# Talking-heads attention with two mixers: the odd key block of the second mix kept whole on one column half, and the first mix put ahead of the score product

## The chip, the cores and the metric

The kernel runs on one core of a Trainium2 chip. The metric is device time in microseconds (us), the time of the slowest core, here the only one. The engines are TensorE (PE, with its weight loads PEld), VectorE (DVE), ScalarE (ACT), GpSimd (POOL) and SyncE (SP), which issues the DMAs.

## The reference

Three stages follow each other, all in float32. The change touches the first alone.

```python
# attention: 2 batches, 12 heads, 448 rows, head size 64; w_pre and w_post are 12 x 12
scores = scale * np.matmul(q, k.transpose(0, 1, 3, 2))
scores = np.einsum('bhij,hg->bgij', scores, w_pre)          # first mix, over heads
scores = scores - np.max(scores, axis=-1, keepdims=True)
attn = np.exp(scores)
attn = attn / (np.sum(attn, axis=-1, keepdims=True) + 1e-09)
attn = np.einsum('bhij,hg->bgij', attn, w_post)             # second mix, over heads
x = np.matmul(attn, v)                                      # then heads side by side: 448 x 768
# mixer 1: u = x + token mixing (448 -> 256 -> 448); x = u + relu(u @ w_ch1) @ w_ch2   (768 -> 1536 -> 768)
# mixer 2: gelu(x @ w_in) in two halves, the second normalised and mixed over tokens,
#          product of the halves @ w_out, plus x
```

## The kernel before, in words

**Attention** takes about the first 190 us. A batch's 448 query rows are cut in four chunks of 120, 120, 120 and 88 rows. A chunk is worked through in steps of 20 rows: 46 steps in all, of which the last of each batch has 10 rows (`ne` is 1 there, else 2). A step's 20 rows are four groups of 5 rows; a group times 12 heads fills 60 partitions. So TensorE is used as four quarters of 64x64: row half (which half of the partitions the operands lie in) times column half (which half of the partitions of PSUM is written). Four matmuls, one for each quarter, run side by side.

For a step i, in the order in which the code writes it (the engines keep this order; a wait holds up all that stands behind it on its engine):

- `qk` (L319): the score product of two heads of the next chunk, 4 matmuls of 448 columns into a PSUM pair of the pool `psM`, which ACT copies to `S`. Six of these are spread over a chunk's steps.
- `b_pre(i + 2)` (L362): the first mix. Its operand `P` comes by DMA out of `S`, turned so that heads lie on partitions (`b_dma`, issued 5 steps ahead). 4 matmuls of 448 columns into the pool `psB`.
- `b_max(i + 2)` (DVE, tile `nm`), `b_norm(i + 1)` (POOL: `rc`, `rr` and two `wt`, w_post scaled by one over the sums).
- `b_post(i)` (L400): the second mix, which also turns the data: the exponentials `E` are the stationary operand, cut in blocks of 64 keys, `wt` (60 columns) the moving one. 448 keys are seven blocks. Blocks 0 to 5 go in twos, one to each column half. For the seventh both column halves do half the heads each: two matmuls of 30 columns where the others have 60. This makes 32 matmuls in a full step.
- `b_exp(i + 2)` (ACT, two activations into `E`), `b_turn(i)` (DVE, in three steps ACT: PSUM to `AT`).
- in some steps `av` (L431), the product of a chunk's `AT` with `v`, for three pairs of heads: 18 matmuls that contract over all 128 partitions, and then 6 that contract over 64 for the seventh key block, whose `AT` and `v` lie on the low half of the partitions for heads 0 to 5 and on the high half for heads 6 to 11. Two bank halves `x` of the PSUM pair take the two groups of heads. ACT and DVE copy the result to `xT`, with an interleaving of rows. There are 16 of these.
- the DMAs, and `pump(1)` (L179): one step of the conversion of later weights, which puts single instructions on ACT, DVE or POOL.

`psM` has two buffers, used in turn by `qk`, `post`, `av` and `xps` (transposes in the last five steps). So a `qk` in a step behind a plain step needs the buffer of the `qk` before it, which is free when ACT has copied that one to `S`.

**The rest** (about 194 us to the end) is the two mixers, dense matmuls in 3-term float32r products; nothing of it changes.

A float32 matmul stands in the trace as two MATMUL records, each with a weight load: 32 matmuls are 64 records.

Of the kernel before, what the change touches and what calls it, by code (L numbers as in the profile page):

```python
# [8 lines left out]
F32 = mybir.dt.float32  # L9
# [5 lines left out]
AF = mybir.ActivationFunctionType  # L15
ALU = mybir.AluOpType
AX = mybir.AxisListType
PSUM = bass.MemoryType.PSUM

LD, LP = 5, 2  # L20
# [10 lines left out]
def tile_kernel(ctx, tc, q, k, v, w_pre, w_post, w_tok1, w_tok2, w_ch1, w_ch2,  # L31
                w_u, w_v, g_ln, w_sg, b_sg, w_out, out):
    nc = tc.nc
    B, D, H, S = 2, 64, 12, 448
    P = 128
    NP = H // 2
# [7 lines left out]
    IB = 10  # L44
    TILES = P // IB
    CH = [(0, 120), (120, 120), (240, 120), (360, 88)]
# [8 lines left out]
    xT = xpool.tile([P, NCC, T], F32, name="xT")  # L55
# [188 lines left out]
    for o in GATE_ORDER.split():  # L244
        j = int(o[1])
# [40 lines left out]
    atp = actx.enter_context(tc.tile_pool(name="atp", bufs=1))  # L286
    ap_ = actx.enter_context(tc.tile_pool(name="attn", bufs=1))
# [12 lines left out]
    NQ = NP // QG  # L300

    def load_v(b, g):
        t = vn[b, g] = ap_.tile([P, 14 * D], F32, tag=f"vn{g}", name=f"vn{b}_{g}")
        nc.sync.dma_start(out=t, in_=v[b, :, g])

    def load_q(b, c, g, eng=nc.sync):
# [55 lines left out]
    def b_pre(i):  # L362
        ne = steps[i][3]
        ps = st[i]["pre"] = pair(f"pre{i}", psB)
        for r, cols in enumerate(HALVES):
            for e in range(ne):
                rs = slice(64 * e, 64 * e + 64 - PAD * e)
                nc.tensor.matmul(ps[cols, e, :S], lhsT=wp[rs], rhs=ring[(2 * i + r) % NP_BUFS][rs], start=True, stop=True)  # L368
# [26 lines left out]
            st[i]["w"].append(wt)  # L395

    AT = {}
    NG = (NK // 2) * H + H // 2

    def b_post(i):  # L400

        b, c, p, ne = steps[i]
        if p == 0:
            AT[b, c] = atp.tile([P, NG, CH[0][1]], F32, tag="AT", name=f"AT{b}_{c}", bufs=2)
        ps = st[i]["ps"] = pair(f"post{i}")
        for e in range(ne):
            E, wt = st[i]["e"][e], st[i]["w"][e]
            for s in range((NK + 1) // 2):
                for x, cols in enumerate(HALVES):
                    t = min(2 * s + x, NK - 1)  # L410
                    w = slice(0, HW) if 2 * s + 1 < NK else slice(x * HW // 2, (x + 1) * HW // 2)
                    o = e * 256 + s * HW
                    for r in range(2):
                        rs = slice(64 * r, 64 * r + HW)
                        nc.tensor.matmul(ps[cols, r, o:o + w.stop - w.start], lhsT=E[rs, t * 64:(t + 1) * 64],  # L415
                                         rhs=wt[rs, w], start=True, stop=True)

    def b_turn(i, copy):

        b, c, p, ne = steps[i]  # L420
        src = st[i]["ps"].rearrange("p r (e x) -> p (r e) x", e=2)[:, ::3 - ne, :NG * HB]
        dst = AT[b, c][:, :, 2 * IB * p:2 * IB * p + 2 * ne * HB]
        dst, src = dst.rearrange("p g (a i) -> p a g i", i=HB), src.rearrange("p a (g i) -> p a g i", i=HB)
        if i < NB - 1:
            copy(dst, src)  # L425
        else:
            nc.scalar.copy(dst[:, :1], src[:, :1])
            nc.vector.tensor_copy(dst[:, 1:], src[:, 1:])
        st[i] = None

    def av(b, c, hps):  # L431

        s0, n = CH[c]
        nb = n // IB
        rest = n - nb * IB
        cols = IB * (nb + (rest > 0))
        NH = NK // 2
        ps = pair(f"av{b}_{c}_{hps[0]}")
        at = AT[b, c]
        sides = [[hp for hp in hps if hp // (NP // 2) == x] for x in range(2)]  # L440

        def into(hp, x, j):
            o = sides[x].index(hp) * cols
            return ps[HALVES[j], x, o:o + cols]

        for x in range(2):
            for hp in sides[x]:
                for s in range(NH):
                    for j in range(2):
                        nc.tensor.matmul(into(hp, x, j), lhsT=vn[b, hp // 2][:, ((hp % 2 * 2 + j) * NH + s) * D:][:, :D],  # L450
                                         rhs=at[:, s * H + 2 * hp + j, :cols], start=(s == 0 and hp == sides[x][0]),
                                         stop=False, skip_group_check=True)
        for m in range(max(map(len, sides))):
            for x in range(2):
                if m < len(sides[x]):
                    hp = sides[x][m]
                    g = hp % (NP // 2)
                    for j in range(2):
                        nc.tensor.matmul(into(hp, x, j), lhsT=vn[b, g][HALVES[x], (4 * NH + j) * D:][:, :D],
                                         rhs=at[HALVES[x], NH * H + 2 * g + j, :cols], start=False, stop=True,  # L460
                                         skip_group_check=True)

        t0 = s0 + b * S
        for hs, x, copy in zip(sides, range(2), (nc.scalar.copy, nc.vector.tensor_copy)):
            dst = xT[:, hs[0]:hs[-1] + 1]
            src = ps[:, x, :len(hs) * cols].rearrange("p (c k) -> p c k", k=cols)
            copy(dst[:, :, t0:t0 + nb * IB].rearrange("p c (i j) -> p c j i", j=nb),
                 src[:, :, :nb * IB].rearrange("p c (j i) -> p c j i", i=IB))
            if rest:
                h = rest // 2  # L470
                copy(dst[:, :, t0 + nb * IB:t0 + n].rearrange("p c (i r) -> p c r i", r=2),
                     src[:, :, nb * IB:].rearrange("p c (r i) -> p c r i", i=HB)[:, :, :, :h])

    CW = C // 2

# [79 lines left out]
    AT_ACT = (-5, -3, 3)  # L555
    TURNS_AT = {(-1, 0), (4, 0), (-3, 1), (-2, 1), (0, 1), (1, 1), (4, 1)}

    AVS = ((0, 1, 3), (2, 4, 5))
    END = NB - LD
    LAST_AV = (0, 1)  # L560
    todo = []
# [299 lines left out]
    banks = {}  # L861
# [53 lines left out]
def layouts(q, k, v, w_pre, w_post, moe_w_tok1, moe_w_tok2, moe_w_ch1, moe_w_ch2,  # L915
# [28 lines left out]
    def spread(a):  # L944

        n = a.shape[-1]
        full, rest = n // 10, n % 10 // 2
        t = np.zeros((*a.shape[:-1], 128), a.dtype)
        rows = t[..., :120].reshape(*a.shape[:-1], 10, 12)
        rows[..., :full] = a[..., :10 * full].reshape(*a.shape[:-1], 10, full)  # L950
        if rest:
            rows[..., :rest, full:full + 2] = a[..., 10 * full:].reshape(*a.shape[:-1], rest, 2)
        t[..., :120] = rows.reshape(*a.shape[:-1], 120)
        return t

    def tokens(w):
# [10 lines left out]
    vr = v.reshape(B, 2, H // 4, 2, S, D)[..., whole:, :].transpose(0, 1, 4, 2, 3, 5).reshape(B, 128, H // 4, 2 * D)  # L967
    vt = np.concatenate([vt.reshape(B, 128, H // 4, -1), vr], -1)
# [57 lines left out]
```

## Time and profile before

| | before |
|---|---|
| runs | 509.75, 505.27, 509.64 us; median 509.64 |
| the profiled execution | 511.61 us, of which the span of the trace is 509.8 |
| PE busy, of the span | 485.2 us, 95% |
| DVE, ACT, POOL busy | 342.6, 236.5, 208.7 us |
| instructions | 14006, of which MATMUL 6010 and LDWEIGHTS 6010 |
| DMA | 63.84 MB, mean 125 GB/s |

The share of busy time is a mean over stages with different limits; the attention has to be read by itself. "Issue" in a list of waits is time in which an engine waited for nothing that the profile shows.

### The profile page before, as it was taken

Reading aid. Unit: us, or ns where it says so; the run is one execution under the profiler, and the core shown is the slowest. Engines: PE = TensorE matmul, PEld = TensorE weight load, DVE = VectorE, ACT = ScalarE, POOL = GpSimd, SP = SyncE. Lnnn points to the kernel's source line nnn. Section 1 sums busy time; section 2 is a strip of 40 time slices with the busy share of each in tenths; the row PEclk is TensorE's granted clock in tenths of the full one; section 3 lists DMA queues with packets and bytes.
Section 4 is the critical chain, followed back from the end, with each engine's and each line's share of the span. In section 5 each row is a group of like instructions: output and inputs, shape, how many; then the busy total and the mean of one; then the engine's idle time right before and its main releaser. Section 6 shows DMA issues by size and latency. Waiting matters only on the chain.

```text
span 509.8 us, 14006 instructions
## 1 busy us (share of the span) xinstructions
PE 485.2 (95%) x6010; PEld 411.8 (81%) x6010; DVE 342.6 (67%) x452; ACT 236.5 (46%) x457; POOL 208.7 (41%) x292
## 2 busy tenths in 40 slices
PE   9987999989799889999999999999999999999997
PEld 5455677756577569999999999999999998888896
DVE  4574566657365645963657687789887964897882
ACT  3675576576466434462434443333332345454320
POOL 2355256365355420284123322444554434258400
PEclk9999999999899999999999999999999999999999
DMA  6788364455523500310234343353432323103122
GB/s 225 231 227 232 139 219 154 153 200 179 171 112 139 205 4 2 125 63 27 98 103 145 125 143 105 123 165 101 149 123 88 119 73 124 32 0 123 68 85 109
DMA packets 26306, 63.84 MB, mean 125 GB/s; under 512 B 2900, under 2 KB 19844, under 8 KB 26244
## 3 DMA queue, kind: packets, MB, share of 16 engines
q1 hardware_dynamic: 26100, 62.75, 37.0%
q8 instruction: 47, 0.77, 0.6%
q10 hardware_dynamic: 144, 0.20, 0.1%
q14 instruction: 15, 0.12, 0.1%
HBM read 40.83 MB, written 2.75 MB: 85 GB/s over the span
## 4 chain that ended last, share of the span: by engine, by line
PE 89%; issue 4%; ACT 2%; DVE 2%; DMA 1%; POOL 1%; SPq 0%; POOLq 0%; ACTq 0%
PE qk L328 8%; PE post L415 8%; PE av L450 6%; PE c1ps L632 6%; PE c2ps L632 6%; PE pre L368 6%; PE c2ps L634 6%; PE c1ps L634 6%; PE c2ps L633 6%; PE c1ps L633 6%; PE ups L633 2%; PE ups L632 2%; PE ups L634 2%; PE vps L634 2%; PE vps L633 2%
## 5 line engine op out<-in xcount | busy, mean ns | idle before, releaser
L156 POOL TENSOR_TENSOR wl<-cv,wh 128x768 fp32r<-128x768 f32 x28 | 52.6, 1878 | 132.0 <-ACT wh L153 100.6
L415 PEld LDWEIGHTS post<-wt,E 60*64 60x64 f32 x2880 | 54.3, 138 | 31.8 <-issue 23.6
L381 ACT ACTIVATE E<-pre,nm 128x448 f32<-128x448 f32 x90 | 56.3, 632 | 37.3 <-DVE nm L373 33.4
L415 PE MATMUL post<-wt,E 60*64 60x60 f32 (+1 forms) x2880 | 56.3, 221 | 10.5 <-issue 8.3
L373 DVE TENSOR_REDUCE nm<-pre 128x2 f32<-128x896 f32 (+1 forms) x46 | 49.1, 1068 | 24.0 <-PE pre L368 22.2
L135 DVE SCALAR_TENSOR_TENSOR cv<-raw,cv 128x768 uint32<-128x768 uint32 (+2 forms) x44 | 53.1, 1207 | 1.2
L328 PE MATMUL qk<-kn,qn 64*64 64x448 f32 x384 | 50.0, 565 | 3.2 <-issue 1.9
L632 PE MATMUL c1ps<-uh,wh 128*128 128x448 f32 x144 | 52.3, 363 | 0.0
L632 PE MATMUL c2ps<-r1h,wh 128*128 128x448 f32 x144 | 52.3, 363 | 0.0
L368 PE MATMUL pre<-P,wp 64*64 64x448 f32 (+1 forms) x360 | 50.7, 547 | 1.7 <-ACT E L381 1.1
L634 PE MATMUL c2ps<-r1h,wl 128*128 128x448 f32 x144 | 52.2, 362 | 0.0
L634 PE MATMUL c1ps<-uh,wl 128*128 128x448 f32 x144 | 52.2, 362 | 0.0
L633 PE MATMUL c1ps<-ul,wh 128*128 128x448 f32 x144 | 51.8, 360 | 0.0
L633 PE MATMUL c2ps<-r1l,wh 128*128 128x448 f32 x144 | 51.8, 360 | 0.0
L425 DVE COPY AT<-post 128x840 f32<-128x840 f32 (+1 forms) x42 | 44.0, 1047 | 9.7 <-PE post L415 9.6
L113 ACT ACTIVATE cv<-raw 128x768 f32<-128x768 f32 (+2 forms) x44 | 36.1, 821 | 26.9 <-POOL wl L156 19.9
L388 POOL TENSOR_SCALAR rc<-sm 128x2 f32<-128x2 f32 (+1 forms) x46 | 10.5, 229 | 90.2 <-ACT E L381 89.7
L333 ACT COPY S<-qk 128x896 f32<-128x896 f32 x42 | 38.0, 905 | 17.4 <-PE qk L328 15.4
L137 DVE SCALAR_TENSOR_TENSOR cv<-raw,cv 128x768 uint32<-128x768 uint32 (+2 forms) x44 | 40.3, 915 | 1.0
L153 ACT CAST wh<-cv 128x768 fp32r<-128x768 f32 x28 | 23.4, 835 | 34.8 <-DVE cv L137 33.9
L655 DVE SCALAR_TENSOR_TENSOR r1l<-c1ps,r1h 128x448 fp32r<-128x448 f32 x24 | 15.0, 624 | 30.6 <-ACT r1h L653 30.6
L450 PE MATMUL av<-AT,vn 128*64 128x120 f32 (+1 forms) x576 | 32.5, 266 | 2.0 <-issue 1.9
(148 smaller groups left out, 1035.3 us busy)
## 6 DMA issues: line engine op xcount, KB each, us to landing
P<-S SPq DMA_DIRECT2D x88, 210.0 KB
raw<-in_w_ch_dram SPq DMA_DIRECT2D x24, 768.0 KB
raw<-in_w_v_dram SPq DMA_DIRECT2D x6, 512.0 KB
raw<-in_w_u_dram SPq DMA_DIRECT2D x4, 768.0 KB
raw<-in_w_out_dram SPq DMA_DIRECT2D x6, 512.0 KB
qn<-in_q_dram SPq DMA_DIRECT2D x15, 192.0 KB
kn<-in_k_dram SPq DMA_DIRECT2D x12, 224.0 KB
vn<-in_v_dram SPq DMA_DIRECT2D x6, 448.0 KB
```

What stands on the lines that cost most here:

```text
L135: nc.vector.scalar_tensor_tensor(fi, lo, 29, fi, op0=ALU.logical_shift_right, op1=ALU.bitwise_or)
L156: nc.gpsimd.tensor_tensor(dst[1], f, f32(dst[0]), op=ALU.subtract)
L328: nc.tensor.matmul(ps[cols, j, :S], lhsT=qn[b, c, i // QG][rows, i % QG, cols], rhs=KX[b, i][rows], start=True, stop=True)
L368: nc.tensor.matmul(ps[cols, e, :S], lhsT=wp[rs], rhs=ring[(2 * i + r) % NP_BUFS][rs], start=True, stop=True)
L373: nc.vector.tensor_reduce(out=st[i]["nm"][:, :ne], in_=st[i]["pre"][:, :ne, :S], axis=AX.X, op=ALU.max, negate=True)
L381: nc.scalar.activation(t, st[i]["pre"][:, e, :S], AF.Exp, bias=st[i]["nm"][:, e:e + 1], scale=1.0, accum_out=sm[:, e:e + 1])
L415: nc.tensor.matmul(ps[cols, r, o:o + w.stop - w.start], lhsT=E[rs, t * 64:(t + 1) * 64], rhs=wt[rs, w], start=True, stop=True)
L425: copy(dst, src)
L450: nc.tensor.matmul(into(hp, x, j), lhsT=vn[b, hp // 2][:, ((hp % 2 * 2 + j) * NH + s) * D:][:, :D], rhs=at[:, s * H + 2 * hp + j, :cols], ...
L632: nc.tensor.matmul(ps, lhsT=lh, rhs=rh, start=(start and i == 0), stop=False)
L633: nc.tensor.matmul(ps, lhsT=lh, rhs=rl, start=False, stop=False)
L634: nc.tensor.matmul(ps, lhsT=ll, rhs=rh, start=False, stop=(stop and i == n - 1))
```

## The change

The second mix: the seventh key block is no longer cut by heads. With `e` for the two halves of a step's rows, block seven of half `e` goes whole (60 columns) to column half `e`; in a step with `ne` of 1, to column half `r`. The matmuls of a full step become 28. `AT` gets a layout of 84 groups of 60 columns (before 42 of 120) of the same size; `b_turn` copies as many elements as before, and in the two short steps splits them between ACT and DVE in four copies.

The product with v: block seven of a pair of heads now lies on the low partitions for half the chunk's rows and on the high ones for the other half. So its 6 matmuls of up to 120 columns become 12 of up to 60. Half of them stand ahead of the 18 full ones (each row half writing one bank half) and half behind (with bank halves exchanged). Between the two a tiny POOL memset (`turned_at`, 128x8) waits for the first ones, and the first of the second ones waits for it. The 18 full matmuls read their moving operand in two runs of 60 columns instead of one of 120. The tile of `v` grows from 14x64 to 16x64 columns, as block seven is stored for both halves. The pairs of heads of the two calls become (0, 1, 2) and (3, 4, 5), ACT always copies two pairs and DVE one, in plain rows; q's columns are ordered differently in memory to fit.

In a step `b_pre(i + 2)` stands ahead of the first `qk`.

```diff
-        t = vn[b, g] = ap_.tile([P, 14 * D], F32, tag=f"vn{g}", name=f"vn{b}_{g}")
+        t = vn[b, g] = ap_.tile([P, 16 * D], F32, tag=f"vn{g}", name=f"vn{b}_{g}")
...
+    turned_at = ap_.tile([P, 8], F32, name="turned_at")
+    NH = NK // 2
+    GM = NH * H
+    NG = 2 * GM + H
...
+        def mix(e, r, x, t, o):
+            rs = slice(64 * r, 64 * r + HW)
+            nc.tensor.matmul(ps[HALVES[x], r, o:o + HW], lhsT=st[i]["e"][e][rs, t * 64:(t + 1) * 64],
+                             rhs=st[i]["w"][e][rs, :HW], start=True, stop=True)
+
         for e in range(ne):
-            E, wt = st[i]["e"][e], st[i]["w"][e]
-            for s in range((NK + 1) // 2):
-                for x, cols in enumerate(HALVES):
-                    t = min(2 * s + x, NK - 1)
-                    w = slice(0, HW) if 2 * s + 1 < NK else slice(x * HW // 2, (x + 1) * HW // 2)
...
+            for s in range(NH):
+                for x in range(2):
                     for r in range(2):
...
+                        mix(e, r, x, 2 * s + x, (e * NH + s) * HW)
+        for r in range(2):
+            for e in range(ne):
+                mix(e, r, e if ne == 2 else r, NK - 1, 2 * NH * HW)
...
+        def rests(turned, fence=None):
+
+            mms = []
+            for m in range(len(sides[0])):
+                for e in range(2):
+                    x = e ^ turned
+                    if m < len(sides[x]):
+                        hp = sides[x][m]
+                        o = m * cols + e * half
+                        for j in range(2):
+                            mms.append(nc.tensor.matmul(
+                                ps[HALVES[j], x, o:o + half],
+                                lhsT=vn[b, hp // 2][HALVES[e], (4 * NH + hp % 2 * 2 + j) * D:][:, :D],
+                                rhs=at[HALVES[e], 2 * GM + 2 * hp + j, :half],
+                                start=(not turned and m == 0), stop=turned, skip_group_check=True))
+            if fence:
+                tc.add_manual_dep(mms[0].ins, fence.ins.name, SYNC, reason="banks change rows")
+            return mms
+
+        mms = rests(False)
+        fence = nc.gpsimd.memset(turned_at, 0.0)
+        for mm in mms[-4:]:
+            tc.add_manual_dep(fence.ins, mm.ins.name, SYNC, reason="banks change rows")
         for x in range(2):
-            for hp in sides[x]:
+            for m, hp in enumerate(sides[x]):
                 for s in range(NH):
                     for j in range(2):
...
+                                         rhs=main[:, :, s * H + 2 * hp + j, :half], start=False, stop=False,
...
+        rests(True, fence)
...
-    AVS = ((0, 1, 3), (2, 4, 5))
+    AVS = ((0, 1, 2), (3, 4, 5))
...
+        if ahead:
+            b_pre(i + LP)
         if due:
             qk(*due.pop(0))
-        if ahead:
-            b_pre(i + LP)
```

The first place is TensorE in step 6 (score product `qk`, first mix `pre` of step 8, second mix `post`). Before:

```order
L328 MATMUL qk_2_5_639<-kn_5_115,qn_2_1_227 64x448 x4
L368 MATMUL pre_645<-P_93,wp 64x448 x2
L368 MATMUL pre_645<-P_94,wp 64x448 x2
L415 MATMUL post_661<-wt_0_594,E_0_568 64x60 x12
L415 MATMUL post_661<-wt_0_594,E_0_568 64x30 x4
L415 MATMUL post_661<-wt_1_596,E_1_570 64x60 x12
L415 MATMUL post_661<-wt_1_596,E_1_570 64x30 x4
```

In the change:

```order
L369 MATMUL pre_616<-P_93,wp 64x448 x2
L369 MATMUL pre_616<-P_94,wp 64x448 x2
L329 MATMUL qk_2_5_621<-kn_5_116,qn_2_1_228 64x448 x4
L413 MATMUL post_638<-wt_0_575,E_0_549 64x60 x12
L413 MATMUL post_638<-wt_1_577,E_1_551 64x60 x12
L413 MATMUL post_638<-wt_0_575,E_0_549 64x60
L413 MATMUL post_638<-wt_1_577,E_1_551 64x60
L413 MATMUL post_638<-wt_0_575,E_0_549 64x60
L413 MATMUL post_638<-wt_1_577,E_1_551 64x60
```

The eight matmuls of 30 columns are gone, four of 60 stand at the end; the score product stands directly ahead of the second mix.

The second place is TensorE behind that second mix, where the product with v follows. Before:

```order
L450 MATMUL av_0_0_700<-AT_0_280,vn_0_123 64x120 x12
L450 MATMUL av_0_0_700<-AT_0_280,vn_1_385 64x120 x6
L459 MATMUL av_0_0_700<-AT_0_280,vn_0_123 64x120 x4
L459 MATMUL av_0_0_700<-AT_0_280,vn_1_385 64x120 x2
L328 MATMUL qk_3_0_736<-kn_0_101,qn_3_0_575 64x448 x4
```

In the change:

```order
L460 MATMUL av_0_0_673<-AT_0_281,vn_0_124 64x60 x2
L460 MATMUL av_0_0_673<-AT_0_281,vn_1_378 64x60 x2
L460 MATMUL av_0_0_673<-AT_0_281,vn_0_124 64x60 x2
L477 MATMUL av_0_0_673<-AT_0_281,vn_0_124 64x120 x12
L477 MATMUL av_0_0_673<-AT_0_281,vn_1_378 64x120 x6
L460 MATMUL av_0_0_673<-AT_0_281,vn_1_378 64x60 x2
L460 MATMUL av_0_0_673<-AT_0_281,vn_0_124 64x60 x4
L369 MATMUL pre_715<-P_95,wp 64x448 x2
```

Six short matmuls stand on each side of the 18, where six long ones stood behind them.

The third place is POOL in the same step, the chain that scales w_post (`rc`, `rr`, `wt`) for the next step and for the one behind it. In the change:

```order
L389 TENSOR_SCALAR rc_629<-sm_608 128x2
L391 TENSOR_TENSOR rr_631<-rc_629,mone 128x2
L395 TENSOR_SCALAR wt_0_633<-wd_post,rr_631 128x60
L395 TENSOR_SCALAR wt_1_635<-wd_post,rr_631 128x60
L470 MEMSET turned_at 128x8
L389 TENSOR_SCALAR rc_729<-sm_667 128x2
```

The memset is new; before, the second `rc` follows the `wt` directly.

## Rows read from the trace of the kernel before

**Rows 1.** Attention: busy us (instructions) of PE, PEld, DVE, ACT, POOL; clock, DMA, GB/s.

```profile
19.30:194.00 174.70, 156.18 (x4274) 116.64 (x4276) 103.54 (x123) 105.17 (x249) 81.37 (x190) 0.97 0.50 164
```

**Rows 2.** Chain that ended last, 145 to 155 us: start, us, what.

```profile
145.49 0.75 PE qk L328 x6
...
147.90 0.78 PE qk L328 x6
148.69 0.75 PE pre L368 x8
...
150.47 0.98 PE qk L328 x8
...
152.20 0.90 PE post L415 x64
153.10 2.00 PE av L450 x36
155.10 0.46 PE av L459 x10
```

**Rows 3.** ACT's timeline, 149 to 153 us: start, us, what, idle before.

```profile
149.51 0.90 ACT L333 COPY S<-qk 128x896 f32<-128x896 f32 x1
150.71 0.63 ACT L381 ACTIVATE E<-pre,nm 128x448 f32<-128x448 f32 x1 [0.30 <-issue]
...
151.95 0.90 ACT L333 COPY S<-qk 128x896 f32<-128x896 f32 x1
```

**Rows 4.** Waits of PE: for what, us in total, times, longest.

```profile
PE post L415 <- issue: 8.3, 8, 3.1
PE av L459 <- issue: 2.1, 3, 1.3
PE av L450 <- issue: 1.9, 2, 1.1
PE qk L328 <- issue: 1.9, 1, 1.9
...
PE qk L328 <- ACT S L333: 1.0, 1, 1.0
```

**Rows 5.** The page's DMA queue of instructions: packets, MB, share of 16 engines.

```profile
q8 instruction: 47, 0.77, 0.6%
```

**Rows 6.** PE between two issue waits: us, busy (matmul records), clock, DMA.

```profile
124.05:128.70 4.65, 3.76 (x127) 1.00 0.86 254
```

**Rows 7.** Second mix (L415), two stretches: us, PE busy (records begun), PEld, clock.

```profile
72.60:72.97 0.37, 0.34 (x24) 0.34 (x24) 1.00 0.87 237
72.60:73.06 0.46, 0.43 (x32) 0.43 (x32) 1.00 0.89 265
```

**Rows 8.** PE's timeline in one product with v.

```profile
87.05 2.07 PE L450 MATMUL av<-AT,vn 128*64 128x120 f32 x36
89.04 0.53 PE L459 MATMUL av<-AT,vn 64*64 64x120 f32 x10
...
89.50 0.92 PE L328 MATMUL qk<-kn,qn 64*64 64x448 f32 x6
```

**Rows 9.** DVE's timeline, 149 to 152 us.

```profile
149.53 1.09 DVE L373 TENSOR_REDUCE nm<-pre 128x2 f32<-128x896 f32 x1 [0.37 <-PE pre L368]
150.54 1.05 DVE L425 COPY AT<-post 128x840 f32<-128x840 f32 x1
```

**Rows 10.** Chain that ended last, 45 to 52 us.

```profile
45.74 3.12 issue
...
50.13 1.56 PE qk L328 x7
```

**Rows 11.** The stretch behind that wait; its granted clock is 0.55.

```profile
48.50:52.30 3.80, 3.44 (x53) 2.51 (x57) 1.06 (x1) 0.57 (x1) 3.03 (x4) 0.55 0.84 242
```

**Rows 12.** POOL's timeline around the product with v of the rows above.

```profile
84.94 1.93 POOL L131 TENSOR_SCALAR cv<-cv 128x512 f32<-128x512 f32 x1
...
88.09 0.60 POOL L394 TENSOR_SCALAR wt<-wd_post,rr 128x60 f32<-128x60 f32 x2
```

More of the change, by code (lines that the diff above doesn't have):

```diff
@@ L17 @@
 AX = mybir.AxisListType
+SYNC = mybir.DependencyInfo(mybir.DependencyClass.Sync, mybir.DependencyReason.DATA)
 PSUM = bass.MemoryType.PSUM
@@ L397, in tile_kernel @@
     AT = {}
-    NG = (NK // 2) * H + H // 2
+    turned_at = ap_.tile([P, 8], F32, name="turned_at")
+    NH = NK // 2
+    GM = NH * H
+    NG = 2 * GM + H
     def b_post(i):
@@ L403, in b_post @@
         if p == 0:
-            AT[b, c] = atp.tile([P, NG, CH[0][1]], F32, tag="AT", name=f"AT{b}_{c}", bufs=2)
+            AT[b, c] = atp.tile([P, NG, CH[0][1] // 2], F32, tag="AT", name=f"AT{b}_{c}", bufs=2)
         ps = st[i]["ps"] = pair(f"post{i}")
+        def mix(e, r, x, t, o):
+            rs = slice(64 * r, 64 * r + HW)
+            nc.tensor.matmul(ps[HALVES[x], r, o:o + HW], lhsT=st[i]["e"][e][rs, t * 64:(t + 1) * 64],
+                             rhs=st[i]["w"][e][rs, :HW], start=True, stop=True)
@@ L406, in b_post @@
         for e in range(ne):
-            E, wt = st[i]["e"][e], st[i]["w"][e]
-            for s in range((NK + 1) // 2):
-                for x, cols in enumerate(HALVES):
-                    t = min(2 * s + x, NK - 1)
-                    w = slice(0, HW) if 2 * s + 1 < NK else slice(x * HW // 2, (x + 1) * HW // 2)
-                    o = e * 256 + s * HW
+            for s in range(NH):
+                for x in range(2):
                     for r in range(2):
-                        rs = slice(64 * r, 64 * r + HW)
-                        nc.tensor.matmul(ps[cols, r, o:o + w.stop - w.start], lhsT=E[rs, t * 64:(t + 1) * 64],
-                                         rhs=wt[rs, w], start=True, stop=True)
+                        mix(e, r, x, 2 * s + x, (e * NH + s) * HW)
@@ L418, in b_turn @@
+        for r in range(2):
+            for e in range(ne):
+                mix(e, r, e if ne == 2 else r, NK - 1, 2 * NH * HW)
     def b_turn(i, copy):
         b, c, p, ne = steps[i]
[L421 to L424, printed above, removed]
+        src = st[i]["ps"][:, :, :NG * HB].rearrange("p r (g i) -> p r g i", i=HB)
@@ L425, in b_turn @@
+        dst = AT[b, c][:, :, 2 * HB * p:2 * HB * p + ne * HB].rearrange("p g (r i) -> p r g i", i=HB)
+        if ne == 2:
             copy(dst, src)
         else:
-            nc.scalar.copy(dst[:, :1], src[:, :1])
-            nc.vector.tensor_copy(dst[:, 1:], src[:, 1:])
+            main = dst[:, 0, :2 * GM].rearrange("p (e g) i -> p e g i", e=2)
+            for r, rows in enumerate(HALVES):
+                copy = (nc.scalar.copy, nc.vector.tensor_copy)[r]
+                copy(main[:, r], src[:, r, :GM])
+                copy(dst[rows, 0, 2 * GM:], src[rows, r, 2 * GM:])
@@ L433, in av @@
         s0, n = CH[c]
[L434 to L437, printed above, removed]
+        half = -(-n // IB) * HB
+        cols = 2 * half
         ps = pair(f"av{b}_{c}_{hps[0]}")
         at = AT[b, c]
[L440 to L444, printed above, removed]
+        main = at[:, :2 * GM].rearrange("p (e g) c -> p e g c", e=2)
@@ new lines, in av @@
+        sides = hps[:-1], hps[-1:]
+        def rests(turned, fence=None):
[15 more added lines that the diff above has]
+            return mms
@@ L446, in av @@
+        mms = rests(False)
+        fence = nc.gpsimd.memset(turned_at, 0.0)
+        for mm in mms[-4:]:
+            tc.add_manual_dep(fence.ins, mm.ins.name, SYNC, reason="banks change rows")
         for x in range(2):
-            for hp in sides[x]:
+            for m, hp in enumerate(sides[x]):
                 for s in range(NH):
                     for j in range(2):
-                        nc.tensor.matmul(into(hp, x, j), lhsT=vn[b, hp // 2][:, ((hp % 2 * 2 + j) * NH + s) * D:][:, :D],
-                                         rhs=at[:, s * H + 2 * hp + j, :cols], start=(s == 0 and hp == sides[x][0]),
-                                         stop=False, skip_group_check=True)
@@ L453, in av @@
[L453 to L460, printed above, removed]
+                        nc.tensor.matmul(ps[HALVES[j], x, m * cols:(m + 1) * cols].rearrange("p (e c) -> p e c", e=2),
+                                         lhsT=vn[b, hp // 2][:, ((hp % 2 * 2 + j) * NH + s) * D:][:, :D],
+                                         rhs=main[:, :, s * H + 2 * hp + j, :half], start=False, stop=False,
@@ L461, in av @@
                                          skip_group_check=True)
+        rests(True, fence)
         t0 = s0 + b * S
         for hs, x, copy in zip(sides, range(2), (nc.scalar.copy, nc.vector.tensor_copy)):
[L465 to L472, printed above, removed]
+            copy(xT[:, hs[0]:hs[-1] + 1, t0:t0 + n],
+                 ps[:, x, :len(hs) * cols].rearrange("p (c k) -> p c k", k=cols)[:, :, :n])
     CW = C // 2
@@ L946, in spread @@
         n = a.shape[-1]
[L947 to L950, printed above, removed]
+        full, rest = n // 10, n % 10
+        a = np.concatenate([a, np.zeros((*a.shape[:-1], -n % 10), a.dtype)], -1)
+        a = a.reshape(*a.shape[:-1], 2, -1, 5)
+        t = np.zeros((*a.shape[:-3], 128), a.dtype)
+        rows = t[..., :120].reshape(*a.shape[:-3], 2, 5, 12)
+        rows[..., :full] = a[..., :full, :].swapaxes(-1, -2)
         if rest:
-            rows[..., :rest, full:full + 2] = a[..., 10 * full:].reshape(*a.shape[:-1], rest, 2)
-        t[..., :120] = rows.reshape(*a.shape[:-1], 120)
+            rows[..., 0, :, full:full + 2] = a[..., full, :].swapaxes(-1, -2)
+        t[..., :120] = rows.reshape(*a.shape[:-3], 120)
         return t
@@ L966, in layouts @@
     vt = vs[..., :whole, :].reshape(B, H // 4, 4, S // 128, 128, D).transpose(0, 4, 1, 2, 3, 5)
-    vr = v.reshape(B, 2, H // 4, 2, S, D)[..., whole:, :].transpose(0, 1, 4, 2, 3, 5).reshape(B, 128, H // 4, 2 * D)
-    vt = np.concatenate([vt.reshape(B, 128, H // 4, -1), vr], -1)
+    vr = vs[..., whole:, :].reshape(B, H // 4, 4, S - whole, D).transpose(0, 3, 1, 2, 4).reshape(B, S - whole, H // 4, -1)
+    vt = np.concatenate([vt.reshape(B, 128, H // 4, -1), np.concatenate([vr, vr], 1)], -1)
     wp = diagonal(w_pre).transpose(0, 1, 3, 2).reshape(2, 64, 60)
```

## The prediction, on record before the changed kernel ran

> **What bounds the kernel now.** I first read the stretches: the attention, 19 to 194 us, is the only part that the change touches, and PE is busy in 156.2 of its 174.7 us, its clock 0.97, with 4274 matmul records and as many loads [rows 1]. So what TensorE saves there counts, if nothing else sets the pace. Next I read the chain that ended last where no accident disturbs it. The reader is to see three steps between two products with v: score product 0.78, first mix 0.75, second mix 0.90, so 2.41 from the first `qk` to the second; the third `qk` takes 0.98 and comes late, and from 145.49 to 153.10 the three steps take 7.61 instead of 7.23 [rows 2]. ACT's timeline tells why: `S` of the second `qk` is copied from 149.51 to 150.41, and the third `qk`, which needs that buffer, begins at 150.47 [rows 2, 3]. Last I read PE's waits: 14.2 us are put down to issue (8.3 + 2.1 + 1.9 + 1.9), the longest 3.1, against 1.0 for `S` [rows 4]. Between two such waits stand 127 matmul records [rows 6] and as many loads, about 256 instructions; and 6010 matmuls with 6010 loads over 47 instruction packets are 256 as well [rows 5]. So PE waits for its program: one packet of about 16 KB for 256 instructions.
>
> **Second mix.** 24 records of 60 columns begin within 0.34 us, the next 8, of 30 columns, take 0.09 [rows 7]. Four go side by side, so a group of four costs 0.057 us with 60 columns and 0.045 with 30. Before, a step has 12 groups of 60 and 4 of 30 (0.68 + 0.18 = 0.86), now 14 of 60 (0.80). The difference is 0.06 to 0.07; with 0.07 and 44 full steps it is **-3.1 us**. The two short steps lose 0.02 each, nothing. The Trainium skill, page "TensorEngine Tiling (Array Packing)", section "Instruction Overhead", says that every matmul carries about 60 cycles, so that a free dimension of 1 costs as much as one of 60, and that a small dimension is not to be cut further. By that rule the 30 columns would have cost 0.057 a group and the step would save two groups, -5.0 us instead of -3.1. The rows stand between.
>
> **Product with v.** The short matmuls behind the 18 long ones take 0.46 us (89.04 to 89.50) [rows 8]. Now there are eight groups of up to 60 columns in place of four of 120: 8 x 0.057 = 0.46, no gain. In addition one more change of place and one wait that is over when PE comes to it; I take one group, 0.07 each, 16 times: **+1.1 us**. The ends are nothing and 0.20, which is what the dearest hand-over of rows 2 costs (0.98 against 0.78): 0 to +3.2. No row shows a moving operand read in two runs. The nearest is a copy of 840 elements in runs of five, 1.05, against 896 in two runs, 0.90 [rows 3, 9]: at most (1.05 - 0.84) / 168 = 1.2 ns a run, 0.7 us over 576 records; I take nothing.
>
> **The order in a step.** I write the three steps of rows 2 down again with the new order, from 0, with the durations of rows 2, 3 and 9 (`S` 0.90, the two activations 1.24 from 150.71 to 151.95, `nm` 1.09, `AT` 1.05, 0.06 to 0.1 from one engine to the next). Step 1: first mix to 0.75, `qk` to 1.53, second mix to 2.36; `S` 1.59 to 2.49, activations to 3.73, `AT` 2.46 to 3.51. Step 2: first mix to 3.11, `qk` to 3.89, second mix to 4.72; `nm` 3.51 to 4.60, `S` 3.95 to 4.85, activations to 6.09, `AT` 4.82 to 5.87. Step 3: `qk` 5.47 to 6.25, `S` 6.31 to 7.21, second mix to 7.08. No `qk` waits any more. But the product with v takes the buffer of the `qk` just ahead, and between them lies now the second mix alone: it waits for `S` until 7.27, some 0.19. So the stretch goes from 7.61 to 7.27; 0.21 of this is the second mix, already counted, 0.13 is the order. There are ten such stretches between the first product with v and the last one before 154 us; in about half of them an issue wait lets ACT catch up anyway, so I count half, -0.7, and most of the 1.0 that `qk` waits for `S` [rows 4], -0.8: **-1.5 us**. Ends: -3 if all stretches gain alike, +2.5 if the new wait is 0.45 everywhere and nothing goes.
>
> **Instructions.** 180 matmuls go (44 x 4 + 2 x 2), 96 come (16 x 6): 84 fewer, 336 instructions with both records and their loads, 1.3 packets. At 1.0 us, the mean of 14 issue waits (14.2 / 14): **-1.3 us**, between -4 and +3.1 (one more wait like the longest), since where packets fall is a matter of luck. The Trainium skill, page "Runtime: NRT & Kernel Launch", section "Instruction fetch mechanics", has blocks of 16 KiB and 256 instructions too, but calls the cost of crossing one mostly hidden. By that this term is nothing and the sum 1.3 us higher; the trace does not agree, with 14.2 us in waits.
>
> **At nothing:** `b_turn` copies as many elements; the copies to `xT` lose their interleaving, and PE does not wait for them; `v`'s 64 KB more a load are 0.4 us at 164 GB/s [rows 1] in transfers issued steps ahead. If that cover is gone, it is 0.4 a load, six times. The split copies of the short steps and the step with two `qk` may cost 0.3 to 0.6 once each; I leave them out.
>
> **Sum:** -3.1 + 1.1 - 1.5 - 1.3 = -4.8. Against the profiled execution, 511.61, that is 506.8; it lies 2.0 above the median of the runs, 509.64, so 504.8, rounded to **505.0**.
>
> **Rivals.**
> - *The program is the bound, more gain.* After the 3.12 us wait the granted clock is 0.55, half the time at the lower of its two levels, 1.2 GHz; `qk` takes 1.56 [rows 10, 11]. If the fewer packets shorten the 3.1 and 1.9 us waits to 1.0 and spare the slow stretches behind them (0.78 for a `qk` alone), another 3.0 + 1.6 us go: about 500.5. For it: they are the largest waits. Against: the DMA share there is 0.8 [rows 11], and the change does not lower that. Chance 0.17.
> - *ACT sets the pace.* `S` and two activations return every 2.44 us (149.51 to 151.95) [rows 3], as long as PE's step. If stretches stay at 7.6, ten times 0.34 do not come: 508.4, and to 510.5 with the upper price of the product with v. For it: the new wait for `S`. Against: the schedule above. Chance 0.17.
> - *The memset comes late: slower.* On POOL it stands behind the scaling of w_post, which in one place ended at 88.69, 1.64 us after the 18 matmuls began, held up by a conversion of 1.93; they last 1.99 [rows 8, 12]. The second short matmuls wait once it ends more than about 2.2 us after that begin, and with them all of PE. If it is 0.7 us late (a third of a conversion) in all 16, +11.2 - 4.8: 516. Against: this is one of the worst of the 16 places, and the conversion of the same step stands behind the memset. Chance 0.11. The Trainium skill, page "TensorEngine Tiling (Array Packing)", section "Gotcha 1: PSUM Pressure", demands such a guard, since different row tiles must not use one bank at once; no run here shows what happens without.
> - The forecast, 503 to 508: 0.55.
>
> **Numbers.** A measurement here can tell 1% from no change, so faster is below 504.5 and slower above 514.7. Faster: the first rival and four tenths of the forecast, 0.17 + 0.22, said 0.40. Slower 0.11. Same 0.49. The range, 500.5 to 510.5, holds the forecast, most of the first rival and the second; it leaves out the third and the ends.
>
> **What would show it.** Right: the second mix some 0.07 shorter in the chain; no `qk` that waits for `S`, and a short wait ahead of the first short matmuls of the product with v; 46 packets; fewer issue waits. Wrong: a PE wait for the memset; products with v of 2.7 us or more; or the stretch between two of them still 7.6.

## The result, and the profile after

| | before | changed |
|---|---|---|
| median of the runs | 508.58 us (5 runs, 505.27 to 509.75) | 501.08 us (5 runs, 500.73 to 501.9) |
| ratio | | 0.9868, 95% interval 0.9827 to 0.991 |
| the profiled execution: time, span | 511.61, 509.8 us | 501.08, 499.3 us |
| mean granted clock in it | 0.990 | 1.000 |
| instructions, of which MATMUL | 14006, 6010 | 13651, 5842 |

The kernel became 7.5 us faster by the medians and 6.7 by the means, which is the 1.3% of the ratio (0.9 to 1.7 by the interval). The range (500.5 to 510.5) holds the time; the forecast's own 503 to 508 does not. The time is that of the first rival (about 500.5), and "within 1%" had been given the larger chance (0.49 against 0.40). The profiled execution of the kernel before is one of its slower ones, so its profile holds more waits and more low clock than its usual run.

All of it comes from the attention. From the first record of the second mix to the first of the mixers it took 175.8 us before and 164.9 after; the rest took 314.4 and 314.6. The stretch that answers to [rows 1], in the changed kernel (columns as there):

```profile
19.70:184.60 164.90, 149.52 (x4138) 109.88 (x4134) 100.68 (x124) 102.73 (x247) 82.45 (x205) 1.00 0.54 175
```

The clock is 1.00 where [rows 1] has 0.97: in that execution some 5 of 174.7 us were missing, and here nothing is. PE's waits in the changed kernel, to be read beside [rows 4]:

```profile
PE post L413 <- issue: 7.2, 7, 2.4
PE av L460 <- ACT S L334: 1.7, 7, 0.5
PE av L477 <- issue: 1.4, 2, 1.1
PE post L413 <- DVE AT L437: 1.3, 1, 1.3
...
PE post L413 <- POOL wt L395: 1.0, 2, 0.5
PE post L413 <- POOL rr L391: 1.0, 1, 1.0
PE pre L369 <- DMA P<-S: 0.9, 2, 0.6
...
PE pre L369 <- ACT E L382: 0.6, 1, 0.6
PE av L460 <- DVE AT L437: 0.4, 1, 0.4
PE xps L496 <- DVE AT L431: 0.4, 1, 0.4
PE post L413 <- ACT S L334: 0.3, 1, 0.3
```

Three things are to be seen. The waits for instructions are 8.6 us instead of 14.2, the longest 2.4 instead of 3.1. The score product no longer waits for `S`; the product with v does, seven times (the longest, 0.49 us at 85 us, stands at a 256th instruction and may be a wait for a packet). And there is no wait for the memset. The queue of instructions has one packet less than in [rows 5]:

```profile
q8 instruction: 46, 0.75, 0.6%
```

The stretch between two products with v that no wait for instructions disturbs, from the chain of waits of the changed kernel (start, us, what; it answers to [rows 2]):

```profile
136.97 2.00 PE av L477 x36
...
142.44 0.73 PE qk L329 x7
143.17 0.80 PE post L413 x53
...
144.00 0.76 PE pre L369 x7
144.76 0.79 PE qk L329 x8
145.56 0.02 issue
145.58 0.91 ACT S L334
146.49 0.04 issue
146.54 0.45 PE av L460 x12
```

The second mix has 0.80 (53 of its 56 records) where [rows 2] has 0.90, and the 18 long matmuls take 2.00 as before, though their moving operand lies in two runs. But the last `qk` is followed by ACT's copy of it and then by `av`: the second mix behind that `qk` is not in the chain, TensorE waits for ACT. From the first record of one `av` to that of the next this stretch takes 10.04 us (136.49 to 146.54); before it took 10.18 (142.86 to 153.03). So where nothing disturbs, a stretch gained 0.14 us, and there are about ten. That is 1 to 2 of the 7.5 us.

The largest single place that both profiles of the kernel before show (the second is e8) is the end of the attention. TensorE's timeline before, from 172 to 187 us (start, us, line, operation, shapes, count, idle before):

```profile
176.17 0.63 PE L459 MATMUL av<-AT,vn 64*64 64x120 f32 x12 [1.35 <-issue]
...
181.86 0.63 PE L459 MATMUL av<-AT,vn 64*64 64x120 f32 x8 [0.41 <-issue]
...
186.91 0.43 PE L415 MATMUL post<-wt,E 60*64 60x60 f32 x16 [1.39 <-issue]
```

and of the changed kernel at the same work:

```profile
170.70 0.63 PE L413 MATMUL post<-wt,E 60*64 60x60 f32 x28 [0.26 <-issue]
...
177.36 0.55 PE L496 MATMUL xps<-ident,xT 128*128 128x128 f32 x3 [0.35 <-DVE AT L431]
...
178.38 0.69 PE L413 MATMUL post<-wt,E 60*64 60x60 f32 x28 [0.47 <-POOL wt L395]
```

From the third-last to the last start of `av` it is 18.0 us before (172.76 to 190.79, 1.1 of it missing in the clock, which is 0.94 there) and 14.5 after (165.85 to 180.31): 3.15 us of waits for instructions became 0.26. The first profile loses more in one other place, from the `av` at 105.34 to that at 142.86 (37.5 us against 32.7 in the changed kernel), but e8 needs 33.7 there.

### The profile page after: what moved, and what is told of

Read it like the earlier page. It is cut to its first block, busy times and chain, and to the rows that moved or that the text cites. A ratio compares the mean times of both kernels' runs of the same rounds, so it can differ in the third digit from the quotient of the medians.

```text
span 499.3 us, 13651 instructions
## 1 busy us (share of the span) xinstructions
PE 477.6 (96%) x5842; PEld 403.6 (81%) x5842; DVE 339.6 (68%) x450; ACT 234.3 (47%) x456; POOL 210.5 (42%) x308
## 4 chain that ended last, share of the span: by engine, by line
PE 84%; ACT 5%; issue 4%; DVE 3%; DMA 1%; POOL 1%; SPq 0%; POOLq 0%; ACTq 0%; DVEq 0%
PE c2ps L646 6%; PE c1ps L646 6%; PE c2ps L648 6%; PE c1ps L648 6%; PE av L477 6%; PE c2ps L647 6%; PE c1ps L647 6%; PE qk L329 6%; PE pre L369 5%; PE post L413 5%; ACT E L382 3%; PE av L460 2%; PE ups L647 2%; PE ups L646 2%; PE ups L648 2%
## 5 line engine op out<-in xcount | busy, mean ns | idle before, releaser
L413 PEld LDWEIGHTS post<-wt,E 60*64 60x64 f32 x2520 | 49.1, 134 | 30.2 <-issue 17.8
L382 ACT ACTIVATE E<-pre,nm 128x448 f32<-128x448 f32 x90 | 56.5, 637 | 14.6 <-DVE nm L374 14.2
L413 PE MATMUL post<-wt,E 60*64 60x60 f32 x2520 | 51.7, 219 | 10.7 <-issue 7.2
L431 DVE COPY AT<-post 128x840 f32<-128x840 f32 x41 | 42.4, 1033 | 19.3 <-PE post L413 19.0
L369 PE MATMUL pre<-P,wp 64*64 64x448 f32 (+1 forms) x360 | 52.3, 545 | 1.7 <-DMA P<-S 0.9
L329 PE MATMUL qk<-kn,qn 64*64 64x448 f32 x384 | 48.5, 540 | 0.1
L391 POOL TENSOR_TENSOR rr<-rc,mone 128x2 f32<-128x2 f32 (+1 forms) x46 | 32.4, 704 | 3.8
```

The source lines that it names most:

```text
L329: nc.tensor.matmul(ps[cols, j, :S], lhsT=qn[b, c, i // QG][rows, i % QG, cols], rhs=KX[b, i][rows], start=True, stop=True)
L382: nc.scalar.activation(t, st[i]["pre"][:, e, :S], AF.Exp, bias=st[i]["nm"][:, e:e + 1], scale=1.0, accum_out=sm[:, e:e + 1])
L413: nc.tensor.matmul(ps[HALVES[x], r, o:o + HW], lhsT=st[i]["e"][e][rs, t * 64:(t + 1) * 64], rhs=st[i]["w"][e][rs, :HW], start=True, stop=True)
```

## The experiments

Three things vary: the **layout** (the seventh block, the product with v), the **order** in a step, and, from e4 on, the **pool** out of which `av` takes its banks. "Stretch" is the last undisturbed one from `av` to `av` with three score products between, "issue" the sum of PE's waits for instructions in the one profiled execution, "clock" the mean over the timed runs. Each ratio is to the kernel before, run on the same chip.

| kernel | layout, order, pool | median us | ratio, 95% interval | stretch | issue | clock |
|---|---|---|---|---|---|---|
| before | old, old, `psM` | 507.6 to 508.6 | 1 | 10.18 | 14.2; e8: 11.7 | 0.993 |
| e1; e9 | old, new, `psM` | 511.55; 510.48 | 1.0075 (1.0029 to 1.012); 1.0031 (0.9984 to 1.0077) | e9: 10.15 | e9: 12.3 | 0.990; 0.992 |
| e5 | old, old, `psB` | 502.78 | 0.9936 (0.9901 to 0.9971) | 10.18 | 6.3 | 0.996 |
| e10 | old, new, `psB` | 504.98 | 0.9951 (0.9913 to 0.9988) | 9.86 | 12.9 | 0.994 |
| e2 | new, old, `psM` | 500.85 | 0.9879 (0.9843 to 0.9915) | 10.17 | 7.4 | 0.998 |
| changed | new, new, `psM` | 501.08 | 0.9868 (0.9827 to 0.991) | 10.04 | 8.6 | 0.997 |
| e6; e12 | new, old, `psB` | 500.54; 498.75 | 0.9867 (0.9828 to 0.9907); 0.9851 (0.9797 to 0.9904) | 10.13; 10.13 | 5.5; 4.1 | 0.996; 0.997 |
| e4; e11 | new, new, `psB` | 497.2; 498.18 | 0.9822 (0.977 to 0.9873); 0.9829 (0.9776 to 0.9882) | e4: 9.61 | 6.2; 4.5 | 0.997; 0.996 |
| e3 | changed, block seven cut | 511.9 | 1.0077 (1.0033 to 1.0121) | 10.22 | 13.2 | 0.992 |
| e7 | e4 without opening rows | 494.84 | 0.9731 (0.9678 to 0.9785) | 9.36 | 6.6 | 0.995 |

**e1 and e2: one half of the change each.** e1 is the kernel before with only the order changed, e2 the changed kernel with only the order put back:

```diff
-        if due:
-            qk(*due.pop(0))
         if ahead:
             b_pre(i + LP)
+        if due:
+            qk(*due.pop(0))
```

Expected of e1: 

> The kernel before with the first mix ahead of the score product and nothing else. Theory A (the order: the score product no longer waits for ACT's copy of S, and the new wait is small): most of the 7.5 us come from here, about 502 to 504 us, no PE wait of the score product for S. Theory B (fewer matmuls and instruction packets: the layout): 507 to 509 us as before, because a PE step is as long as before and 14 us of issue waits stay.

Expected of e2: 

> The changed kernel with the score product ahead of the first mix again, so the layout alone. Theory A: 506 to 509 us, the step of the second mix shorter by 0.07 but the score product waiting for S again. Theory B: 501 to 503 us, with issue waits of about 9 us instead of 14.

Measured: the order alone is 0.75% slower, not faster, outside both theories; the layout alone gives the whole gain, 7.6 us by the medians and 1.2% by the ratio, which is theory B (0.15 us below its range). One of e1's twelve executions, the profiled one, took 2687 us and is not read; e9 repeats it. That the layout gains in e2 is not a matter of pace: its stretch is 10.17, that of the kernel before. The chain of e2, at the same place, shows what sets it:

```profile
145.66 1.34 ACT E L382 x4
147.00 0.80 ACT S L334
147.81 0.04 issue
147.85 0.98 PE qk L329 x8
148.84 0.75 PE pre L369 x8
149.59 0.81 PE post L413 x56
```

The activations, then the copy of `S`, then the third `qk`, as in [rows 2, 3]: with the old order ACT sets the pace, and what the second mix saves ends up in `qk`'s wait. What e2 has less than before are waits for instructions (7.4 us against 14.2 and 11.7) and missing clock (0.998 against 0.993 in the timed runs).

**e3: the matmuls of block seven cut in two again**, all else as in the changed kernel:

```diff
-        def mix(e, r, x, t, o):
+        def mix(e, r, x, t, o, f=0, n=HW):
...
-                mix(e, r, e if ne == 2 else r, NK - 1, 2 * NH * HW)
+                mix(e, r, e if ne == 2 else r, NK - 1, 2 * NH * HW, 0, HW // 2)
+        for r in range(2):
+            for e in range(ne):
+                mix(e, r, e if ne == 2 else r, NK - 1, 2 * NH * HW, HW // 2, HW // 2)
```

Expected: 

> The changed kernel with each 60-column matmul of the seventh key block cut into two of 30 columns in the same quarter: 32 matmuls in a step as before, all else as changed. Theory A: 0.07 us a step, 44 times, if nothing absorbs it: 501 + 3 = 504 us, issue waits as in the changed kernel. Theory B: 2.8 instruction packets more, so issue waits go back to about 14 us and the time to 506 or more.

Measured: 10.8 us slower than the changed kernel, more than the change gained; this is theory B. 180 matmuls, 720 instructions, three packets (49) were added. The second mix alone in e3 and in the changed kernel (us, PE busy and records, PEld, clock, DMA):

```profile
146.83:147.82 0.99, 0.99 (x64) 0.99 (x64) 1.00 0.20 69
```

```profile
142.93:143.80 0.87, 0.87 (x56) 0.87 (x56) 1.00 0.24 91
```

The eight records more take 0.12 us, whatever their width. 45 times 0.12 are 5.4 us. The waits for instructions grow by 4.6 us (13.2 against 8.6), with one of 2.7 at the end of the attention, where the changed kernel has 0.26; one stretch of low clock comes back. `av` no longer waits for `S` here, and PE's other waits are 2.5 us less (5.1 against 7.6); the spans differ by 8.2.

**e4: `av` in the pool of the first mix.**

```diff
-        ps = pair(f"av{b}_{c}_{hps[0]}")
+        ps = pair(f"av{b}_{c}_{hps[0]}", psB)
```

Expected: 

> The changed kernel with the product with v in the PSUM pool of the first mix, whose buffer has long been free: the wait for ACT's copy of S ahead of it, 0.4 us from the last record of the second mix in seven to ten places, goes. If PE's own work sets the pace there: 3 to 4 us less, 497 to 498 us. If ACT's chain of S and activations sets it: the wait turns up again at the next step, 500 to 501 us.

Measured: 497.2 us, 3.9 less than the changed kernel by the medians, 2.3 by the ratios, whose intervals overlap; it is the fastest of those that compute everything, and the same kernel as e11 gave 498.18. The wait of `av` for `S` is gone from the list, and TensorE's timeline has `av` right behind the second mix, while `S` is still being copied (from 120.65 to 121.55):

```profile
119.48 0.99 PE L329 MATMUL qk<-kn,qn 64*64 64x448 f32 x8
120.41 1.04 PE L413 MATMUL post<-wt,E 60*64 60x60 f32 x56
121.24 0.44 PE L460 MATMUL av<-AT,vn 64*64 64x60 f32 x12
```

The stretch is 9.61, 0.43 less than in the changed kernel; ten of them are 4.3 us. So the wait is enough to account for what the time shows. PE waited for the memset once here, 0.5 us, in a short chunk; so it did in e11.

**e5, e6 and e10: the pool without the rest.** The same line in the kernel before (e5), in e2 (e6) and in e1 (e10). The expectations call that pool "the pool that the first and second mix use"; it is the first mix's alone.

Expected of e5: 

> The kernel before with one line changed: the product with v takes its banks from the pool that the first and second mix use, as in the run before this one. Theory W (the wait of av for the copy of S is made by the change, whose order sets av right behind a score product): before has no such wait among its waits of TensorE, so the edit brings 0 to -1 us: 507.5 to 508.6. Rival P (the other pool is the better one in any order): as much as in the changed kernel, about -4: 504.5.

Expected of e6: 

> The kernel of e4 with the old order within a step (qk ahead of pre). Theory O (the order of the change is worth what the prediction's term says, and e2 did not show it since the new order pays for it with the wait of av): 498.7 to 500 (1.5 to 2.6 us slower than e4's 497.2; 2.6 us is what qk waits for the copy of S in e2). Rival N (the order is worth nothing by itself): 497.2 within 1.

Expected of e10: 

> The old layout with the new order, and av in the other pool: the last corner of layout, order and pool. Theory W: without av's wait the order pays, about as between e6 and e4 (-2.6 us in the profiles' spans): 2 to 4 us under e5's 502.8, so 499 to 501. Rival N (the order does nothing at either layout): 502.8 within 1.

Measured: e5 is 0.64% faster than the kernel before, 3.2 us (1.5 to 5.0 by the interval), though its stretch is 10.18 like that one's. So its gain isn't the wait of `av`, and theory W does not hold there; the time is rival P's or better. Why the pool helps there was not tested; what its profile shows are waits for instructions of 6.3 us. e6 has the stretch of e2 and its time, 0.5 us above theory O's range and outside rival N's. e10 fell neither to 499 nor stayed at e5's time: its stretch is 9.86, as the theory of the wait has it, but its waits for instructions are 12.9 us and it is 2.2 us slower than e5.

**e7: half of the short matmuls left out.** The kernel of e4 without the opening short matmuls of the product with v and without the memset.

```diff
-        mms = rests(False)
-        fence = nc.gpsimd.memset(turned_at, 0.0)
-        for mm in mms[-4:]:
-            tc.add_manual_dep(fence.ins, mm.ins.name, SYNC, reason="banks change rows")
...
-                                         rhs=main[:, :, s * H + 2 * hp + j, :half], start=False, stop=False,
+                                         rhs=main[:, :, s * H + 2 * hp + j, :half], start=(m == 0 and s == 0), stop=False,
...
-        rests(True, fence)
+        rests(True)
```

Expected: 

> The kernel of e4 without the first half of the short matmuls of the product with v (half of the odd last block's part of that product is left out) and without the memset that divides the two halves: 6 short matmuls less in each of 16 products, 96 in all, 384 instructions. Theory V (the short matmuls lie bare on the path: 0.38 us each time from the first to the first long one in the changed kernel): 16 x 0.3 to 0.38 = -4.8 to -6, and 1.5 packets of instructions at 1 to 2 us: 489 to 491. Rival H (they fill the time until the copy of AT or another wait, which then shows): 494 to 497.

Measured: 494.84 us, which is in rival H's range, 2.4 less than e4 by the medians; by the ratios to the kernel before on each chip (0.9731 against 0.9822) it is 4.6 less, near theory V, and the intervals overlap. So the times do not decide. The stretch is 0.25 shorter, between the two theories: six matmuls in one `av` are three groups of four records at 0.058 and a hand-over.

**e8: the kernel before, profiled once more.**

Expected: 

> The kernel before, profiled once more. If the waits for instructions belong to the program, they come at the same places in TensorE's instructions (each 256th) with about the same sum (14.2 us in the first profile) and with the same stretches of low granted clock; if they depend on the execution, the places stay, but lengths and sum change by some us and the low clock falls elsewhere.

Measured: 510.08 us; 11.7 us of waits for instructions and a clock of 0.989. The places repeat (each 256th instruction of TensorE), and so do most lengths behind 80 us; the large ones at 45 to 54 us do not: one of 3.1 became two, of 1.9 and 2.8, and one of 1.9 at 134 us is gone. The end repeats in full, with 1.6, 0.4 and 1.7 us. So the places belong to the program, and part of the lengths to the execution.

**e9, e11 and e12: the order again**, e11 and e12 (the kernels of e4 and e6) on one chip.

Expected of e9: 

> The kernel of e1 once more (the old layout, with the first mix ahead of the score product), since e1's profile cannot be read. Theory W (the order takes away the score product's wait for the copy of S and hands the product with v a wait of 0.3 to 0.5 us for it, 16 times): the trace shows av waiting for S and qk not, and the time is that of before within 1%: 505 to 512. Rival I (e1's +3.8 us is from more waits for instructions): its waits for instructions sum to 3 us more than before's 11.7 to 14.2.

Expected of e11: 

> The kernel of e4 on the same chip as e12, so that the order's worth is compared in one place. Theory W: 496.5 to 498, 2.5 to 3.5 us under e12. Rival N: equal to e12 within 1.

Expected of e12: 

> The kernel of e6 on the same chip as e11. Theory W: 500 to 501, 2.5 to 3.5 us above e11. Rival N: equal to e11 within 1.

Measured: e9 is within the error of before, as theory W had it; its `qk` waits for `S` no more and its `av` does, but twice (0.9 us in all) and not 16 times. Its waits for instructions, 12.3 us, are not more than before's, so rival I doesn't hold, and e1's 0.75% stays unexplained. e11 and e12 differ by 0.6 us, so theory W, which asked for 2.5 to 3.5, is not borne out by the time, though the last undisturbed stretch is shorter where the new order stands with `psB` (9.61 against 10.13; 9.86 against 10.18). By the ratios (0.01 is 5.1 us) the new order makes +3.8 and +1.6 us (e1 and e9 against before), +0.8 (e10 against e5), -0.6 (the change against e2), -1.1 (e11 against e12) and -2.3 (e4 against e6). Each has an error of 2 to 4 us, which only e1 exceeds, and only e1, e9 and e11 are compared on one chip.

## Why the prediction was right or wrong

**Second mix: mis-sized, -3.1 against -5.4.** A group of four records of 30 columns was priced at 0.045 from a window that ends inside the second mix [rows 7]. But a whole second mix before takes 0.93 for 64 records (before, the same columns), not the 0.86 to which these prices add up:

```profile
149.30:150.23 0.93, 0.93 (x64) 0.93 (x64) 1.00 0.61 231
```

That is 0.058 for each of 16 groups: what the narrow ones seem to save, the group behind them loses. The chain with its 0.90 [rows 2] stood beside the sum and spoke against it. The Trainium skill, page "TensorEngine Tiling (Array Packing)", section "Instruction Overhead", was right here: below 60 columns a matmul costs as much as with 60. The prediction quoted it with its -5.0 and took the row instead; e3, where two groups of 30 columns more take 0.12, and the window above agree with the page.

**Product with v: mis-sized, +1.1 against about +3.** From its first record to the first record of the next step that is no longer mixed with it it takes 2.70 us (136.49 to 139.19), before 2.47 (142.86 to 145.33): 0.2 in each of 16, the upper end of the range of that term, and about the 2.7 that the prediction had named as a sign of being wrong. Before:

```profile
142.86 2.07 PE L450 MATMUL av<-AT,vn 128*64 128x120 f32 x36
...
145.33 0.92 PE L328 MATMUL qk<-kn,qn 64*64 64x448 f32 x6
...
153.03 0.73 PE L450 MATMUL av<-AT,vn 128*64 128x120 f32 x9
```

Changed:

```profile
136.49 0.30 PE L460 MATMUL av<-AT,vn 64*64 64x60 f32 x2
...
139.19 0.93 PE L369 MATMUL pre<-P,wp 60*64 60x448 f32 x6
...
145.28 1.05 PE L413 MATMUL post<-wt,E 60*64 60x60 f32 x56
146.54 0.45 PE L460 MATMUL av<-AT,vn 64*64 64x60 f32 x12 [0.21 <-ACT S L334]
```

The hand-overs between short and long matmuls cost more than one group; e7 has 0.25 for the opening ones. Two runs in the moving operand cost nothing, as taken.

**Order (-1.5): in the stretch as forecast, in the time not shown.** By the same lines the three steps, up to the next `av`, took 7.70 us before (145.33 to 153.03) and take 7.35 now (139.19 to 146.54). That is 0.35 less, where the schedule had 0.34 (7.61 to 7.27). e2, the layout alone, has 7.51 at this place (142.71 to 150.22), so 0.19 came with the layout and 0.16 with the order; the schedule had 0.21 and 0.13. Inside it errors cancel. The three second mixes are 0.12 shorter each and not 0.07, though with the old order part of that goes into `qk`'s wait. The new wait was put at 0.19 and costs 0.43: the last second mix with the wait takes 1.26 (145.28 to 146.54), in e4, which has no wait, 0.83 (120.41 to 121.24). (The 0.21 of the list counts from the modelled end of the last matmul.) In the schedule `S` starts 0.84 after the begin of `qk`, in the trace 1.06 after it (144.52 to 145.58). So the second rival, that the stretches stay as long, did not come true for the steps: ACT sets the pace at their end alone, and that only 0.14 is left from `av` to `av` is the product with v.

The other half of the term, `qk`'s wait of 1.0 for `S`, went as forecast, but at the same place, a short step, the second mix now waits 1.3 us for its split copies (`AT` L437 in the list above), which the prediction had left out at 0.3 to 0.6. From `av` to `av` this place takes 11.03 us (92.80 to 103.83), before 10.69 (94.65 to 105.34). And in the times no comparison shows a gain by the order that is clear of the error.

**Instructions: the mechanism right, its size wrong, and with it the place of the gain.** A packet's share at 1.0 us gave -1.3. In the two profiles it is -5.6 (14.2 to 8.6), and the clock gives about as much again: 0.97 to 1.00 over 175 us is up to 5.2 us. With -5.4 for the second mix, +3 for the product with v and +2.8 for the other waits of PE in the attention (7.6 against 4.8 us), the sum is -10.4; the attention lost 10.9. The timed runs show less, since the profiled execution of before lies 3.0 above its median: the mean clocks of the timed runs, 0.993 and 0.997, are about 2 us apart over 505. With 2 in place of 5.2 the sum is -7.2, near the 7.5 of the medians; but the 14.2 is of that execution too, and with e8's 11.7 it would be -4.7. This is near to the first rival, at 0.17 under-rated: fewer and shorter waits, and the stretches of low clock behind them spared, as [rows 10, 11] show one. That stretch was misread as half the time at the lower level: a clock of 0.55 over 3.8 us is nine tenths of it. The rival's argument against, that the DMA share is as high as before, was true (0.54 against 0.50 over the attention) and no obstacle, since waits also went at the end, where the DMA share is 0.16 to 0.21.

**The range.** That it holds the time is in part luck: -2.3 for the second mix and +1.9 for the product with v nearly cancel, and the instructions gave more than was counted.

**What is open.** The waits do not go by packets alone. Five profiles with the old count (47 to 49 packets, e3 among them) have 11.7 to 14.2 us, the seven with 44 to 46 have 4.1 to 8.6; but e5, with 47, has 6.3. At the end of the attention, behind 160 us, the count does divide them: the six profiles with 47 to 49 packets have 1.9 to 4.0 us there (e3, with the new layout, 2.7), the seven others at most 0.33. All 106 waits of over 0.15 us that the 13 profiles put down to issue stand at the same place of each 256 of TensorE's instructions. So by how much one waits depends on what stands at that place and on when its packet came, and a shift by a few instructions can move some us. Whether the change gained by having fewer instructions or by having them elsewhere was not told apart: for that, instructions would have to be added that take no time of TensorE's.

**The rest.** The memset cost nothing in the changed kernel, as forecast; the third rival did not come true.

## What to carry to other kernels

Price a group of instructions over a whole stage and see that the prices add up to the stage's own row; a window that ends inside it puts the hand-over on the wrong side. When a buffer is shared by work of two kinds, a new order moves the wait for it to whoever takes the buffer next: here one line that gave `av` another pool was worth about 2 to 4 us on top, while no run shows that the order by itself is worth anything in the time. And in a kernel of small matmuls count instructions as a resource of their own: 180 small matmuls cost 10.8 us, of which their time on TensorE is half; waits for instructions are most of the other half.

## What the runs showed of the hardware

**A wait for instructions ends 1.2 to 1.9 us after its packet lands.** The longest one of the changed kernel, in TensorE's timeline:

```profile
44.20 0.64 PE L413 MATMUL post<-wt,E 60*64 60x60 f32 x22
47.28 0.73 PE L413 MATMUL post<-wt,E 60*64 60x60 f32 x33 [2.44 <-issue]
```

and the DMA queue of instructions between 44.60 and 45.80 us:

```profile
q8 instruction: 1, 0.02, 5.4%
```

The packet starts at 44.69, when TensorE is running dry, and lands at 45.72; TensorE goes on at 47.28. In 13 profiles all 86 idle times of over 0.4 us ahead of a matmul at such a place end so, and where TensorE waited less or not at all, the packet had landed at least 1.09 us before. So what decides is when the packet starts: with a flight of 1.0 us as here, some 2 to 3 us ahead of need costs nothing (an estimate from these figures). In the attention it starts from 0.6 us before to 5.7 us after TensorE has passed the place before, here 5.0 after it; why so differently no run shows. The Trainium skill, page "Runtime: NRT & Kernel Launch", section "Instruction fetch mechanics", has the crossing mostly hidden; of 32 to 35 crossings in the attention 2 to 13 cost over 0.4 us, by profile, so most are hidden and the rest is what counts here.

**Low clock follows some of the waits.** In the 13 profiles the granted clock falls to the lower of its two levels, 1.2 GHz, 14 times in the attention, each time within a wait of 1.4 to 3.7 us at a 256th instruction or at most 2.9 us behind its end. But 17 of the 31 waits of that size have none behind them, so a wait spared does not always spare low clock. In the three sets of timed runs of the kernel before (23, 29 and 17) a mean clock lower by 0.01 goes with 7, 5 and 2 us more. The kernels with 11.7 to 14.2 us of waits for instructions have mean clocks of 0.992 to 0.994, the others with a profile 0.995 to 0.998. In a single execution the two can part: e10's profile has 12.9 us of waits at a clock of 1.000, e7's 6.6 us at 0.993.
